# One more block product in seven smaller ones, and block sums carried in PSUM, in a mixer's channel layer

## The chip, the cores and the metric

The kernel runs on one core of a Trainium2 chip. Times are microseconds (us) of the device for one execution. The core has a matrix engine (TensorE, PE in the profile; its loading of the stationary operand is the row PEld), a vector engine (VectorE, DVE), a scalar engine (ScalarE, ACT), GpSimd (POOL) and SyncE (SP), which here only issues transfers (SPq is its queue). Matrix products are written into PSUM, which the program uses as four pairs of banks; a pair holds 128 rows of 1024 numbers. The other engines copy or add from there into SBUF.

## The reference, cut to what matters

```python
attn = ...                                        # attention within hash buckets, 4 x 8 heads, 768 rows of 64
x = attn.transpose(0, 2, 1, 3).reshape(4, 768, 512)
h = np.maximum(x.transpose(0, 2, 1) @ w_tok1, 0.0) @ w_tok2     # token mixing: 768 -> 256 -> 768
u = x + h.transpose(0, 2, 1)
h2 = np.maximum(u @ w_ch1, 0.0) @ w_ch2                         # channel mixing: 512 -> 1536 -> 512
return u + h2
```

Everything is in 32 bit floats. The change lies in the first product of the channel mixing, u @ w_ch1: 3072 rows of 512, to 1536 channels, and in the work around it.

## The kernel before

**Stages.** Attention, token mixing and channel mixing follow each other. The channel stage is the function `channels`. Its data lie turned: channels on the partitions, the 3072 rows of u along the free axis, in XT. They are treated in three column groups s = 0, 1, 2 of 1024 columns (two halves of TT = 512). For each group a hidden stage computes max(u @ w_ch1, 0) into four tiles R[0] to R[3], and then `outputs(s)` (L1260) computes the second product from R and stores it.

**Block products.** Each matrix product is cut in 2 x 2 blocks and done with seven block products in place of eight (the scheme of Strassen and Winograd): p1 and p2 to p7 are products of sums of left blocks (weights) with sums of right blocks (data), and the four results are sums of them:

- r0 = p1 + p2
- r1 = (p1 + p6) + p5 + p3
- r2 = (p1 + p6) + p7 + p4
- r3 = (p1 + p6) + p7 + p5

Sums of weights are made once and kept, in SW1 for the first product; sums of data are made by `inputs` (L601) into T[0] to T[3] (tiles TA and TB) for each group.

**The hidden stage of group 0** is `hidden(0, t)`, t = 0 to 5, one level of this. Between its steps run jobs that `prepare` (L1060) lists: VectorE makes sums of blocks of the weights for a second level, which SP stores in DRAM, in `hidden_passed` for the first product and `passed` for the second.

**The hidden stage of groups 1 and 2** is `hidden_pair(s, t, between)` (L932), t = 0, 1, 2 (GP = 3). Each takes a pair of row blocks, t and t + 3, of each of the two halves of the hidden channels. p1 and p5 are whole there: 4 products of 512 columns each (2 row blocks, 2 steps of depth, `whole`). p2, p6, p7, p3 and p4 are done on a second level, each with seven products of 128 x 128 by 128 x 256, by the class `Smaller` (L893). It has four parts:

- `one`: one product into a bank, and a copy of it into the first quarter of a tile e by ScalarE (L904)
- `three`: three products that go on top of what a bank pair holds already (or open it, where `start` is true)
- `rest`: three more in the bank of `one`
- `finish`: a copy of one product's sum by ScalarE to u (L925), and two sums by VectorE (L927, 128x512, and L930, 128x256), which fill the other three quarters of e

So a block product is a sum of two parts: one lies in the bank pair that `three` wrote, the other in e. The left operands of these seven come from `hidden_passed`, 448 KB for one block product of one pair (`fetch_hidden_left`, L862, issued on SP's queue as soon as the tile has been used for the pair before). The right ones are the raw blocks and four sums that a job of `right_sums` (L838) makes on VectorE, four subtractions of 128x256. They are made once per group: p2's and p6's ahead of the stage, the others at t = 0 in the list `between`.

ScalarE copies bank pairs out (`copy`, L960, 128x1024), VectorE adds (`plus`, L963), ScalarE applies the Relu to r0, r2 and r3 (L966), and r1 gets it in `bounded_minus` (L795), which also makes the difference r1 - r0 that the second product needs. The last of these lie in a list, which `end_rows` (L797) runs during the next pair.

**Looks.** `look` (L1338) belongs to a safety test of q and k. It fetches one 128x768 tile by POOL (L1355, 384 KB), and for the tile fetched some looks before it runs a square (L1344) and a bounded sum (L1345) on ScalarE. There are 36 in all; 12 in the hidden stage of each of groups 1 and 2 (four a pair), and one in each product of `outputs` of groups 0 and 1 (L1226).

**What sets the order.** The order of instructions is written out by hand (`tc.manual_schedule()`): each engine runs its instructions in the order of the code. An instruction waits for others through the tiles that both use. A PSUM tile here is a bank pair, and waits are made for the parts of it that two instructions touch, by bank. `ring` says which bank pair plays which part in a pair of rows, and `ahead` holds the bank pair in which the next step's first products have been begun: p1's of the next pair, or, at the end of a group's hidden stage, the first 8 of 12 depth steps of half of the whole product of `outputs` (`whole_first`, EARLY). That product (`whole_product`, L1182) is the first of `outputs`, 24 products of 256 columns.

The end of a pair, and the beginning of the next, read

```python
            if t + 1 < GP:
                ahead.append(bank_pair(y))
                opened(ahead[0], [0], t=t + 1)
```

where y is the bank pair from which `plus(r[1], banks(Y), rows(u))` reads p5 and p3.

**POOL and SP.** POOL issues the fetches of the looks and the stores of the results, which add to what is in DRAM (L1270). SP issues the fetches of the left operands, and `residual` (L1323) after t = 0, four transfers of 512 KB from XT to the output.

Of the kernel before, what the change touches and what calls it, by code (L numbers as in the profile page):

```python
# [48 lines left out]
def kernel(  # L49
# [702 lines left out]
    def channels(pool, psum, SW1, second, TA, judge):  # L752
# [85 lines left out]
        def right_sums(name, s):  # L838


            sl = [slice(TT * (2 * s + i), TT * (2 * s + i) + TT) for i in range(2)]
            src = {"p2": XT[:, KC:, sl[0]], "p3": XT[:, KC:, sl[1]], "p6": T[1], "p7": T[2], "p4": T[3]}[name]
            if name == "p7":
                z = SW1[:, 1].rearrange("p k c -> p (k c)")[:, : 2 * TT]
            else:
                z = XT[:, ["p2", "p6", "p3", "p4"].index(name), : 2 * TT]
            z = split4(z)
            half = [slice(0, TT // 2), slice(TT // 2, TT)]
            b = [src[:, k, n] for k in range(2) for n in half]

            def job():
                nc.vector.tensor_tensor(z[:, 0], b[1], b[0], op=ALU.subtract)
                nc.vector.tensor_tensor(z[:, 1], b[3], b[1], op=ALU.subtract)
                nc.vector.tensor_tensor(z[:, 2], b[3], z[:, 0], op=ALU.subtract)
                nc.vector.tensor_tensor(z[:, 3], b[2], z[:, 2], op=ALU.subtract)

            return job, [*b, *(z[:, i] for i in range(4))]
# [12 lines left out]

        def hidden_left_at(h):

            h, n = h % 5, 7 * P
            if h < 3:
                return WC1[:, KC:].rearrange("p k c -> p (k c)")[:, n * h : n * h + n]
            return SW1[:, 2 * (h - 3)].rearrange("p k c -> p (k c)")[:, :n]
# [5 lines left out]
        def first_weight(name):  # L882

            return {
                "p2": WC1[:, KC:, : DCH // 2], "p3": SW1[:, 2], "p4": WC1[:, KC:, DCH // 2 :], "p6": SW1[:, 0],
                "p7": SW1[:, 1],
            }[name]
# [5 lines left out]
        class Smaller:  # L893


            def __init__(self, h, name, s):
                self.h, self.w = h, hidden_left_at(h).rearrange("p (i c) -> p i c", i=7)
                self.b = right_sums(name, s)[1]

            def one(self, pair, e):  # L900

                self.ps, self.e = pair, split4(e)
                self.mm(pair[:, 0, : TT // 2], 4, 0)
                nc.scalar.copy(self.e[:, 0], pair[:, 0, : TT // 2])  # L904

            def three(self, pair, start=False):

                self.mm(pair[:, 0, : TT // 2], 5, 2, start)
                self.mm(pair[:, 0, TT // 2 :], 3, 3, False)
                self.mm(pair[:, 1, : TT // 2], 6, 7, start)  # L910

            def rest(self):

                self.mm(self.ps[:, 1, : TT // 2], 0, 4)
                self.mm(self.ps[:, 1, TT // 2 :], 1, 5)
                self.mm(self.ps[:, 0, : TT // 2], 2, 6, False)
                fetch_hidden_left(self.h + 5)

            def mm(self, ps, left, right, start=True):
                accumulate(ps, lambda k: self.w[:, left], lambda k: self.b[right], [0], start)  # L920

            def finish(self):

                u = extra_flat()[:, TT // 2 * (self.h % 2) : TT // 2 * (self.h % 2) + TT // 2]
                nc.scalar.copy(u, self.ps[:, 0, : TT // 2])  # L925
                p57 = self.ps[:, 1].rearrange("p (n t) -> p n t", n=2)
                nc.vector.tensor_tensor(  # L927
                    self.e[:, 1:3], p57, u[:, None, :].to_broadcast([P, 2, TT // 2]), op=ALU.add,
                )
                nc.vector.tensor_tensor(self.e[:, 3], p57[:, 0], self.e[:, 2], op=ALU.add)  # L930

        def hidden_pair(s, t, between):  # L932


            sl = [slice(TT * (2 * s + i), TT * (2 * s + i) + TT) for i in range(2)]
            ks = range(KC)
            r = [a[:, :, t::GP].rearrange("p n i c -> p i n c") for a in R]
            x, z, e, y = ring
            ring[:] = [y, e, z, x]

            p1, e2 = [output_at(i).rearrange("p i n -> p (i n)") for i in (0, 2)]
            p5, e6, u = copies(), copies(), copies()
            e3, e4 = [output_at(i).rearrange("p i n -> p (i n)") for i in (3, 1)]
            e7 = q1.rearrange("p i n -> p (i n)")
            h = 5 * GP * (s - 1) + 5 * t
            p2, p6, p7, p3, p4 = [Smaller(h + i, name, s) for i, name in enumerate(SMALLER)]

            def rows(a):
                return a.rearrange("p (i n c) -> p i n c", i=2, n=2)

            def banks(a):
                return a.rearrange("p i (n c) -> p i n c", n=2)

            def whole(pair, left, right, which=(0, 1), t=t):
                for i in which:
                    at = P * (t + GP * i)
                    accumulate(pair[:, i], lambda k: left(k)[:, at : at + P], right, ks)

            def copy(to, pair):
                nc.scalar.copy(to.rearrange("p (i n) -> p i n", i=2), pair)  # L960

            def plus(to, a, b):
                nc.vector.tensor_tensor(to, a, b, op=ALU.add)  # L963

            def relu(i):
                nc.scalar.activation(r[i], r[i], ACT.Relu)  # L966

            def opened(pair, which, s=s, t=t):
                start = TT * 2 * s
                whole(pair, lambda k: WC1[:, k], lambda k: XT[:, k, start : start + TT], which, t)  # L970

            X = ahead.pop() if ahead else None
            if not X:
                X = bank_pair(x)
                opened(X, [0])
            opened(X, [1])
            Z, E = bank_pair(z), bank_pair(e)
            p2.one(E, e2)
            copy(p1, X)
            p2.three(Z, True)  # L980
            Y = bank_pair(y)
            whole(Y, lambda k: WC1[:, k, DCH // 2 :], lambda k: T[0][:, k], [0])
            n = TT * 3 // 2
            plus(p1[:, :n], Z.rearrange("p i n -> p (i n)")[:, :n], p1[:, :n])
            for job in between[:2]:
                job()
            end_rows()
            p2.rest()
            whole(Y, lambda k: WC1[:, k, DCH // 2 :], lambda k: T[0][:, k], [1])
            p2.finish()  # L990
            copy(p5, Y)
# [3 lines left out]
            copy(u, X)  # L995
            look()
            V = bank_pair(e)
            p7.three(V, True)
            p6.rest()
            plus(p5[:, :n], V.rearrange("p i n -> p (i n)")[:, :n], p5[:, :n])  # L1000
            p6.finish()
            for job in between[2:]:
                job()
# [7 lines left out]
            relu(0)  # L1011
# [10 lines left out]
            if t + 1 < GP:  # L1022
                ahead.append(bank_pair(y))
                opened(ahead[0], [0], t=t + 1)
            else:
                ahead.append(blocks(1)[0])
                whole_first(s, ahead[0])
# [5 lines left out]
            look()  # L1033

            def end():
                relu(3)
                relu(2)
                for i in range(2):
                    bounded_minus(r[1][:, i], r[0][:, i])

            unfinished.append(end)


# [3 lines left out]
        ahead, EARLY = [], [k for k in range(HC) if k % GP < GP - 1]  # L1047
# [12 lines left out]
        def prepare():  # L1060
# [42 lines left out]
            def hidden_parts(name):  # L1103
# [6 lines left out]

            sums = weight_sums(WC2, SW2, slice(0, HC), slice(HC, NHT), low, high)
            return [
                [hidden_parts("p7")], sums, [whole("p1"), second_parts("p7")], *([second_parts(name)] for name in ("p6", "p3", "p5", "p2", "p4")),
                [hidden_parts("p2")], [hidden_parts("p6")], [hidden_parts("p3")], [hidden_parts("p4")],
# [59 lines left out]
        def whole_part(s, pair, m, ks, start=True, stop=True):  # L1174
            w, right = first_left(s), R[int(RIGHT["p1"][1])]
            accumulate(
                split(pair[:, m]), lambda k: w[:, k, P * m : P * m + P], lambda k: right[:, :, k], ks, start, stop,
            )

        def whole_first(s, pair):  # L1180
            whole_part(s, pair, 0, EARLY, stop=False)

        def whole_product(s):
            if ahead:
                pair = ahead.pop()
                whole_part(s, pair, 1, EARLY, stop=False)
                late = [k for k in range(HC) if k not in EARLY]
                for m in (1, 0):
                    whole_part(s, pair, m, late, False)
            else:  # L1190
                pair = blocks(1)[0]
                for m in range(KC):
                    whole_part(s, pair, m, range(HC))
# [4 lines left out]
        def product(s, j, name, q, between, final=None):  # L1198
# [27 lines left out]
            if s < last:  # L1226
                look()
# [165 lines left out]
        for s in range(1, last + 1):  # L1393
            right_sums("p6", s)[0]()
            for t in range(GP):
                hidden_pair(s, t, [right_sums(name, s)[0] for name in ("p7", "p3", "p4")] if t == 0 else [])
                if t == 0:
                    residual(s)
# [8 lines left out]
    def with_token_weights(stage):  # L1407
        with tc.tile_pool(name="tok", bufs=1, reuse_waits="tile") as tok:
# [10 lines left out]
            f"p{i}": dram.tile([P, 8, NHT // 4 * P], F32, name=f"hidden_left{i}") for i in (2, 3, 4, 6, 7)  # L1419
# [102 lines left out]
```

## Time and profile before

| What | us |
|---|---|
| median of 3 runs (793.72 to 794.22) | 794.18 |
| the profiled execution | 793.64 |
| its span, first to last instruction | 791.9 |
| attention | up to about 309 |
| token mixing | 309 to 387 |
| channel mixing | 387 to 792 |

The span is 1.7 us shorter than the profiled execution, which is itself 0.54 us below the median. The granted clock of TensorE is 0.999 over the span.

In what follows, a line of the timeline gives the start, the duration, the engine, the line of the code, the operation and its operands as out<-in with shapes; xN means N records that ran without a break. One product in 32 bit floats leaves two records. Where the engine had been idle, brackets at the end give that time and what ended it. A line of the groups gives the count, then the busy time in us and the mean duration of one in ns, and then the idle time ahead of these and what ended it. The chain of waits is the work that ended last, followed back from the end, here in order of time: start, duration, engine and line.

Three stretches of group 1's hidden stage, as windows of the trace. The columns are the stretch, its length, the busy time of PE, PEld, DVE, ACT and POOL with their instructions, the granted clock, the share of the DMA engines and GB/s:

```profile
525.00:547.50 22.50, 22.15 (x86) 15.98 (x85) 19.14 (x34) 12.54 (x23) 3.67 (x5) 1.00 0.86 241
547.50:569.50 22.00, 22.00 (x87) 16.36 (x87) 18.05 (x25) 16.68 (x29) 2.11 (x5) 1.00 0.90 288
569.50:591.50 22.00, 22.00 (x85) 15.96 (x84) 17.68 (x25) 16.57 (x29) 2.08 (x5) 1.00 0.60 177
```

### The profile page before, as it was taken

To read this page: it belongs to the slowest core of one execution; us is meant where nothing else is said; L and a number is where in the kernel's file an instruction comes from. 1 tells how busy PE (TensorE), PEld (TensorE's weight loads), DVE (VectorE), ACT (ScalarE), POOL (GpSimd) and SP (SyncE) were. 2 spreads that over 40 slices of the span, in tenths; PEclk is the share of its full clock that TensorE was granted. 3 is DMA by queue.
4 is the path that set the end of the run, shared out by engine and by line. 5 is a ranking of instruction groups with operands and counts; after the bars stand their busy time and mean duration, and the time that the engine had idled before them with its cause. 6 is when DMAs were issued, how large, how long until landed. Compare 5 with 4: busy or idle time off the path is not lost.

```text
span 791.9 us, 12326 instructions
## 1 busy us (share of the span) xinstructions
PE 784.5 (99%) x4697; PEld 471.3 (60%) x4697; DVE 674.5 (85%) x921; ACT 442.4 (56%) x718; POOL 53.5 (7%) x77
## 2 busy tenths in 40 slices
PE   9999999999999999999999999999999999999997
PEld 5444444444444444455544458877777887676886
DVE  5989898988987677999697689898879998888996
ACT  6788888888888886333323221327764335775111
POOL 1000000000000000011121010011100012000001
PEclk9999999999999999999999999999999999999999
DMA  4435353537452425795686995798856588650665
GB/s 164 163 123 163 123 163 123 163 127 240 154 180 83 151 44 168 219 264 107 119 280 235 346 333 163 202 294 238 264 163 208 180 219 190 211 171 1 195 166 123
DMA packets 99760, 143.01 MB, mean 181 GB/s; under 512 B 30120, under 2 KB 69744, under 8 KB 99696
## 3 DMA queue, kind: packets, MB, share of 16 engines
q1 hardware_dynamic: 91536, 117.19, 45.6%
q0 software_dynamic: 7728, 24.64, 14.0%
q8 instruction: 38, 0.62, 0.3%
q10 hardware_dynamic: 432, 0.34, 0.2%
q14 instruction: 26, 0.21, 0.1%
HBM read 99.96 MB, written 34.73 MB: 170 GB/s over the span
## 4 chain that ended last, share of the span: by engine, by line
PE 97%; DVE 2%; ACT 1%; issue 0%; DVEq 0%
PE b L780 48%; PE sc L353 20%; PE acc L407 16%; PE t L653 5%; PE t L693 5%; PE sums L431 2%; PE hp L301 1%; PE idle L470 0%; DVE R L963 0%; DVE c L963 0%; PE hw L325 0%; ACT looked L1345 0%; ACT c L960 0%; ACT looked L1344 0%; DVE c L927 0%; DVE q L927 0%
## 5 line engine op out<-in xcount | busy, mean ns | idle before, releaser
L360 ACT ACTIVATE e<-sc 128x768 f32<-128x768 f32 x192 | 154.2, 812 | 10.5 <-PE sc L353 10.1
L353 PE MATMUL sc<-qk 64*128 64x384 f32 x768 | 152.7, 483 | 0.0
L780 PE MATMUL b<-R,second 128*128 128x256 f32 (+1 forms) x612 | 151.2, 404 | 0.0
L780 PEld LDWEIGHTS b<-R,second 128*128 128x128 f32 x612 | 116.2, 190 | 30.8 <-issue 16.5
L786 ACT COPY c<-b 128x512 f32<-128x512 f32 (+1 forms) x78 | 37.4, 488 | 169.3 <-PE b L780 155.5
L407 PE MATMUL acc<-e,vn 128*32 128x384 f32 x1536 | 127.0, 486 | 0.0
L392 DVE TENSOR_TENSOR esd<-esd,e 128x768 f32<-128x768 f32 x96 | 92.0, 958 | 10.4 <-ACT e L360 0.5
L407 PEld LDWEIGHTS acc<-e,vn 128*32 128x32 f32 x1536 | 49.9, 110 | 73.9 <-issue 73.3
L353 PEld LDWEIGHTS sc<-qk 64*128 64x128 f32 x768 | 68.2, 187 | 41.2 <-issue 36.0
L780 PE MATMUL b<-XT,WC 128*128 128x256 f32 (+1 forms) x228 | 75.4, 470 | 0.7 <-DVE R L963 0.7
L353 PE MATMUL sc<-bits 64*128 64x384 bf16 x384 | 62.6, 323 | 0.0
L780 PEld LDWEIGHTS b<-XT,WC 128*128 128x128 f32 x228 | 43.2, 190 | 28.4 <-issue 22.2
L388 DVE SCALAR_TENSOR_TENSOR esd<-e 128x768 f32<-128x768 f32 x32 | 30.6, 956 | 23.3 <-ACT e L360 23.3
L780 PE MATMUL b<-XT,SW 128*128 128x256 f32 (+1 forms) x156 | 43.7, 412 | 0.0
L780 PE MATMUL b<-TA,WC 128*128 128x512 f32 (+1 forms) x108 | 43.6, 521 | 0.0
L653 PE MATMUL t<-x,W 128*128 128x512 f32 x96 | 41.8, 593 | 0.0
L353 PEld LDWEIGHTS <-bits 64*128 64x128 bf16 x384 | 18.7, 94 | 33.1 <-issue 8.8
L780 PEld LDWEIGHTS b<-XT,SW 128*128 128x128 f32 x156 | 29.6, 190 | 11.7 <-issue 6.8
L713 POOL DMA_DIRECT2D XT<-second x8 | 9.9, 1232 | 382.7 <-DVE second L712 355.1
L452 ACT COPY rec<-rec 32x384 f32<-32x384 f32 x64 | 32.6, 510 | 5.0 <-DVE rec L446 4.2
L413 ACT ACTIVATE num<-acc,vsum 128x384 f32<-128x384 f32 x32 | 18.6, 582 | 29.7 <-PE acc L407 29.3
L395 DVE TENSOR_TENSOR esd<-esd,e 128x768 f32<-128x768 f32 x32 | 30.5, 954 | 1.9
(226 smaller groups left out, 1155.8 us busy)
## 6 DMA issues: line engine op xcount, KB each, us to landing
second<-left SPq DMA_DIRECT2D x20, 768.0 KB
raw<-in_moe_w_ch SPq DMA_DIRECT2D x16, 768.0 KB
qk<-in_qk SPq DMA_DIRECT2D x15, 768.0 KB
second<-left SPq DMA_DIRECT2D x18, 576.0 KB
seen<-in_qk POOLq DMA_DIRECT2D x21, 384.0 KB, 4.3
WC<-hidden_left SPq DMA_DIRECT2D x18, 448.0 KB
vn<-in_v SPq DMA_DIRECT2D x16, 384.0 KB
vt<-in_vT SPq DMA_DIRECT2D x16, 384.0 KB
```

The costliest lines, as they stand in the source:

```text
L353: nc.tensor.matmul(sc[:, i, :HALF], t[rows, 1, P * c : P * c + P], t[rows, 0, qs], start=start, stop=not start,)
L360: nc.scalar.activation(e, sc[:, :, :HALF], ACT.Exp, scale=SCALE)
L388: nc.vector.scalar_tensor_tensor(self.d, es[0], NR * EPS, es[1], op0=ALU.add, op1=ALU.add,)
L392: nc.vector.tensor_tensor(self.d, self.d, e, op=ALU.add)
L395: nc.vector.tensor_tensor(self.d, self.d, self.es[-1], op=ALU.add)
L407: nc.tensor.matmul(acc[D * i + d : D * i + d + 32], vn[:, i, c, d : d + 32], e[:, i], start=(c == 0), stop=(c == NR - 1),)
L413: nc.scalar.activation(nums[self.n][:, self.half], acc, ACT.Identity, scale=-1.0, bias=vsum,)
L452: nc.scalar.copy(rec[other : other + 32, h], rec[at : at + 32, h])
L653: nc.tensor.matmul(ps, W1[:, r, P * j : P * j + P], x[:, r], start=(r == 0), stop=(r == NR - 1),)
L693: nc.tensor.matmul(ps[at], left, right, start=start, stop=True, skip_group_check=True,)
L780: nc.tensor.matmul(ps, left(k), right(k), start=start and k == ks[0], stop=stop and k == ks[-1], skip_group_check=True,)
L786: nc.scalar.copy(c, ps)
```

## The change

- In the pairs t = 1 and t = 2 of groups 1 and 2, p5 is done on the second level too, in seven products of 256 columns in place of four of 512. Three of its left operands are raw blocks of the weights; four sums are made by a new job of `prepare`, `fifth_parts`, during group 0, stored in a new piece of `hidden_passed`, and fetched by `fetch_fifth` (256 KB). Its right sums are made by one more `right_sums` job, at t = 0.
- These two pairs have a new order (`hidden_pair`). A sum of block products is written back into PSUM, and later products go on top of it: VectorE writes (p1 + p6) + e5, 128x1024, into the bank pair Y, on which `p5.three` and later `p3.three` accumulate. ScalarE writes the first quarter of p7's e into the bank pair V (in `one`) and, from SW1, the two middle quarters (128x512, at the end of `finish`), VectorE writes the last quarter there; `p7.three` and later `p4.three` accumulate on that. Y is copied to v after `p5.three` (`copy_pair`), and r3 is V + v.
- The pair t = 0 keeps its order as `hidden_first`, but p4's right sums move ahead of `p7.three`, and those of p5 come after the sum of p5 and p7. `end_rows` leaves it.
- `finish` takes its u from three places in turn, not two. Left operands are fetched anew after the second use of a tile, by `used`.
- The whole product of `outputs` is no longer begun in the hidden stage: `whole_part`, `whole_first` and EARLY go.
- The looks are spread otherwise: 4, 3 and 2 in the three pairs of a group, one per product in `outputs(0)` and two in `outputs(1)`; 36 as before.

The diff, cut to its core:

```diff
+            src = {"p2": XT[:, KC:, sl[0]], "p3": XT[:, KC:, sl[1]], "p5": T[0], "p6": T[1], "p7": T[2], "p4": T[3]}[name]
+            if name == "p5":
+                z = left_at(7 * s)[:, HC * 2 * P : HC * 2 * P + 2 * TT]
+            elif name == "p7":
                 z = SW1[:, 1].rearrange("p k c -> p (k c)")[:, : 2 * TT]
...
+        def fetch_fifth(s, t):
+
+            if t < GP:
+                nc.sync.dma_start(
+                    out=fifth_left().rearrange("p (i c) -> p i c", i=4),
+                    in_=hidden_passed["p5"][:, :, P * t : P * t + P],
+                )
+
+        def fifth_left():
+            return SW1[:, 1].rearrange("p k c -> p (k c)")[:, 2 * TT : 2 * TT + 4 * P]
+
...
+            def __init__(self, h, name, s, t):
+                self.h, self.s, self.t, self.fetched = h, s, t, False
                 self.b = right_sums(name, s)[1]
+                if name == "p5":
+                    raw = [a for b in weight_quarters(first_weight(name)) for a in b]
+                    raw = [raw[i][:, 0, P * t : P * t + P] for i in (0, 1, 3)]
+                    sums = fifth_left().rearrange("p (i c) -> p i c", i=4)
+                    self.left = [*(sums[:, i] for i in range(4)), *raw]
+                else:
+                    w = hidden_left_at(h).rearrange("p (i c) -> p i c", i=7)
+                    self.left = [w[:, i] for i in range(7)]
 
             def one(self, pair, e):
 
-                self.ps, self.e = pair, split4(e)
-                self.mm(pair[:, 0, : TT // 2], 4, 0)
-                nc.scalar.copy(self.e[:, 0], pair[:, 0, : TT // 2])
+                self.ps, self.e = split4(pair.rearrange("p i n -> p (i n)")), split4(e)
+                self.mm(self.ps[:, 0], 4, 0)
+                nc.scalar.copy(self.e[:, 0], self.ps[:, 0])
 
             def three(self, pair, start=False):
 
                 self.mm(pair[:, 0, : TT // 2], 5, 2, start)
                 self.mm(pair[:, 0, TT // 2 :], 3, 3, False)
                 self.mm(pair[:, 1, : TT // 2], 6, 7, start)
+                self.used()
 
             def rest(self):
 
-                self.mm(self.ps[:, 1, : TT // 2], 0, 4)
-                self.mm(self.ps[:, 1, TT // 2 :], 1, 5)
-                self.mm(self.ps[:, 0, : TT // 2], 2, 6, False)
-                fetch_hidden_left(self.h + 5)
+                self.mm(self.ps[:, 1], 0, 4, False)
+                self.mm(self.ps[:, 2], 1, 5)
+                self.mm(self.ps[:, 0], 2, 6, False)
+                self.used()
+
+            def used(self):
+
+                if self.fetched and self.h is None:
+                    fetch_fifth(self.s, self.t + 1)
+                elif self.fetched:
+                    fetch_hidden_left(self.h + 5)
+                self.fetched = True
 
             def mm(self, ps, left, right, start=True):
-                accumulate(ps, lambda k: self.w[:, left], lambda k: self.b[right], [0], start)
-
-            def finish(self):
-
-                u = extra_flat()[:, TT // 2 * (self.h % 2) : TT // 2 * (self.h % 2) + TT // 2]
-                nc.scalar.copy(u, self.ps[:, 0, : TT // 2])
-                p57 = self.ps[:, 1].rearrange("p (n t) -> p n t", n=2)
+                accumulate(ps, lambda k: self.left[left], lambda k: self.b[right], [0], start)
+
+            def finish(self, middle=None):
+
+                u = extra_flat()[:, TT // 2 * finished[0] : TT // 2 * (finished[0] + 1)]
+                finished[0] = (finished[0] + 1) % 3
+                nc.scalar.copy(u, self.ps[:, 0])
+                to = self.e[:, 1:3] if middle is None else split(middle)
                 nc.vector.tensor_tensor(
-                    self.e[:, 1:3], p57, u[:, None, :].to_broadcast([P, 2, TT // 2]), op=ALU.add,
+                    to, self.ps[:, 1:3], u[:, None, :].to_broadcast([P, 2, TT // 2]), op=ALU.add,
                 )
-                nc.vector.tensor_tensor(self.e[:, 3], p57[:, 0], self.e[:, 2], op=ALU.add)
+                nc.vector.tensor_tensor(self.e[:, 3], self.ps[:, 1], to[:, 1], op=ALU.add)
+                if middle is not None:
+                    nc.scalar.copy(self.e[:, 1:3], to)
...
+        def open_next(bank, s, t):
+            ahead.append(bank_pair(bank))
+            opened(ahead[0], [0], s, t + 1)
+
+        def later(r, which):
+
+            def end():
+                for i in which:
+                    relu(r[i])
+                for i in range(2):
+                    bounded_minus(r[1][:, i], r[0][:, i])
+
+            unfinished.append(end)
+
...
+        def hidden_first(s, t, between):
...
             X = bank_pair(x)
             opened(X, [0, 1], s, t)
             fetch_fifth(s, t + 1)
...
             for job in between[:2]:
                 job()
-            end_rows()
             p2.rest()
...
             look()
             V = bank_pair(e)
+            between[2]()
             p7.three(V, True)
             p6.rest()
             plus(p5[:, :n], flat(V)[:, :n], p5[:, :n])
+            between[3]()
             p6.finish()
-            for job in between[2:]:
-                job()
             plus(u, u, e6)
...
             p4.one(bank_pair(x), e4)
             look()
             nc.scalar.copy(r[2][:, 1, 1], rows(u)[:, 1, 1])
-            if t + 1 < GP:
-                ahead.append(bank_pair(y))
-                opened(ahead[0], [0], t=t + 1)
-            else:
-                ahead.append(blocks(1)[0])
-                whole_first(s, ahead[0])
+            open_next(y, s, t)
             p4.rest()
...
             look()
+            later(r, (3, 2))
...
+        def hidden_pair(s, t):
+
+
+            r, (p2, p6, p7, p3, p4) = parts_of(s, t)
+            p5 = Smaller(None, "p5", s, t)
+            one, two, three, four = ring
+            e2, e4, e5, e3 = [flat(output_at(i)) for i in range(4)]
+            e6 = flat(q1)
+            p1, u, v = copies(), copies(), copies()
+            n = TT * 3 // 2
+
+            X = ahead.pop()
+            p2.one(bank_pair(three), e2)
+            opened(X, [1], s, t)
+            p6.one(bank_pair(two), e6)
+            copy_pair(p1, X)
+            p2.rest()
+            p6.rest()
+            p2.finish()
+            p6.three(X)
+            p6.finish()
+            look()
+            p5.one(bank_pair(three), e5)
+            plus(u, flat(X), e6)
+            Z = bank_pair(four)
+            p2.three(Z, True)
+            plus(p1[:, :n], flat(Z)[:, :n], p1[:, :n])
+            V = bank_pair(four)
+            p7.one(bank_pair(two), flat(V))
+            p5.rest()
+            p5.finish()
+            p3.one(bank_pair(one), e3)
+            Y = bank_pair(three)
+            plus(flat(Y), e5, u)
+            p7.rest()
+            p7.finish(flat(SW1[:, 0])[:, 7 * P : 7 * P + TT])
+            if t + 1 < GP:
+                look()
+            plus(r[0], rows(p1), rows(e2))
+            p3.rest()
+            p3.finish()
+            p5.three(Y)
+            copy_pair(v, Y)
+            p7.three(V)
+            p4.one(bank_pair(two), e4)
+            relu(r[0])
+            plus(r[3], banks(V), rows(v))
+            p3.three(Y)
+            p4.rest()
+            relu(r[3])
+            plus(r[1], banks(Y), rows(e3))
+            p4.finish()
+            look()
+            p4.three(V)
+            plus(e4, e4, u)
+            end_rows()
+            plus(r[2], banks(V), rows(e4))
+            if t + 1 < GP:
+                open_next(one, s, t)
+            else:
+                ring[:] = [one, three, two, four]
+            later(r, (2,))
...
+            def fifth_parts():
+                (a00, a01), (a10, a11) = weight_quarters(first_weight("p5"))
+                n = QC * P
+                pieces = [flat(q1)[:, : 2 * n], pool.tile([P, S], F32, name="looked", tag="looked", bufs=1)]
+                new = [a[:, n * i : n * i + n].rearrange("p (k c) -> p k c", k=1) for a in pieces for i in range(2)]
+                nc.vector.tensor_tensor(new[1], a00, a10, op=ALU.subtract)
+                nc.vector.tensor_tensor(new[0], a10, a11, op=ALU.add)
+                nc.vector.tensor_tensor(new[2], new[0], a00, op=ALU.subtract)
+                nc.vector.tensor_tensor(new[3], a01, new[2], op=ALU.subtract)
+                for i, a in enumerate(pieces):
+                    to = hidden_passed["p5"].rearrange("p i c -> p (i c)")
+                    nc.sync.dma_start(out=to[:, 2 * n * i : 2 * n * i + 2 * n], in_=a[:, : 2 * n])
+
...
-                [hidden_parts("p2")], [hidden_parts("p6")], [hidden_parts("p3")], [hidden_parts("p4")],
+                [hidden_parts("p2"), fifth_parts], [hidden_parts("p6")], [hidden_parts("p3")], [hidden_parts("p4")],
...
+        def whole_product(s):
+            pair = blocks(1)[0]
             w, right = first_left(s), R[int(RIGHT["p1"][1])]
-            accumulate(
-                split(pair[:, m]), lambda k: w[:, k, P * m : P * m + P], lambda k: right[:, :, k], ks, start, stop,
-            )
-
-        def whole_first(s, pair):
-            whole_part(s, pair, 0, EARLY, stop=False)
-
-        def whole_product(s):
-            if ahead:
-                pair = ahead.pop()
-                whole_part(s, pair, 1, EARLY, stop=False)
-                late = [k for k in range(HC) if k not in EARLY]
-                for m in (1, 0):
-                    whole_part(s, pair, m, late, False)
-            else:
-                pair = blocks(1)[0]
-                for m in range(KC):
-                    whole_part(s, pair, m, range(HC))
+            for m in range(KC):
+                accumulate(
+                    split(pair[:, m]), lambda k: w[:, k, P * m : P * m + P], lambda k: right[:, :, k], range(HC),
+                )
...
-            if s < last:
+            for _ in range(min(s + 1, 2) if s < last else 0):
                 look()
...
-            for t in range(GP):
-                hidden_pair(s, t, [right_sums(name, s)[0] for name in ("p7", "p3", "p4")] if t == 0 else [])
-                if t == 0:
-                    residual(s)
+            hidden_first(s, 0, [right_sums(name, s)[0] for name in ("p7", "p3", "p4", "p5")])
+            residual(s)
+            for t in range(1, GP):
+                hidden_pair(s, t)
```

## The prediction

> **What bounds the kernel now.** I read the head of the page, then the chain of waits in order of time, then the timeline around its breaks.
>
> ```profile
> span 791.9 us, 12326 instructions
> PE 784.5 (99%) x4697; PEld 471.3 (60%) x4697; DVE 674.5 (85%) x921; ACT 442.4 (56%) x718; POOL 53.5 (7%) x77
> ```
>
> TensorE is busy for 99% of the span. A product removed is worth its time only if no other engine is then late.
>
> ```profile
> 386.83 148.42 PE b L780 x482
> ...
> 541.26 1.14 DVE c L963
> 543.46 1.14 DVE R L963
> ...
> 544.65 121.83 PE b L780 x492
> ```
>
> This is the channel stage's chain: one stretch of TensorE up to 535 us, then ScalarE and VectorE until 544.65, then TensorE for 122 us. The break returns in the third column group (675.88) and nowhere else. The timeline shows it:
>
> ```profile
> 535.54 1.02 ACT L960 COPY c<-b 128x1024 f32<-128x1024 f32 x1
> 536.45 0.86 ACT L1344 ACTIVATE looked<-looked 128x768 f32<-128x768 f32 x1
> 536.64 0.96 DVE L963 TENSOR_TENSOR c<-b,c 128x768 f32<-128x768 f32 x1 [1.54 <-ACT c L960]
> ...
> 538.27 0.35 ACT L925 COPY second<-b 128x256 f32<-128x256 f32 x1
> ...
> 538.65 0.69 DVE L927 TENSOR_TENSOR c<-b,second 128x512 f32<-128x512 f32 x1 [1.06 <-ACT second L925]
> ...
> 541.18 1.22 DVE L963 TENSOR_TENSOR c<-c 128x1024 f32<-128x1024 f32 x1
> ...
> 543.38 1.21 DVE L963 TENSOR_TENSOR R<-b,c 128x1024 f32<-128x1024 f32 x1
> ...
> 543.71 0.59 PE L780 MATMUL b<-TB,SW 128*128 128x256 f32 x2
> ...
> 544.65 1.98 PE L780 MATMUL b<-XT,WC 128*128 128x512 f32 x4 [0.35 <-DVE R L963]
> ```
>
> PE's product of 543.71 is done with its slot at 544.14 (0.43 us), and the next starts at 544.65: 0.5 us lost, because the sum into R reads the bank that p1 of t=1 opens. VectorE was late although it had idled 1.54 and 1.06 us just before. One look holds ScalarE for 1.82 us (536.45 to 538.27). The prices, grouped by shape in the channel stage:
>
> ```profile
> L780 PE MATMUL b<-XT,SW 128*128 128x256 f32 x132 | 32.4, 379 | 0.0
> L966 ACT ACTIVATE R<-R 128x1024 f32<-128x1024 f32 x18 | 18.9, 1061 | 3.7 <-DVE R L963 3.7
> L927 DVE TENSOR_TENSOR second<-b,second 128x512 f32<-128x512 f32 x18 | 12.3, 686 | 4.5 <-ACT second L925 4.5
> L960 ACT COPY c<-b 128x1024 f32<-128x1024 f32 x12 | 12.2, 1017 | 8.1 <-PE b L780 8.1
> L930 DVE TENSOR_TENSOR second<-b,second 128x256 f32<-128x256 f32 x18 | 7.6, 424 | 0.6
> L963 DVE TENSOR_TENSOR c<-c 128x1024 f32<-128x1024 f32 x6 | 7.3, 1223 | 0.1
> L963 DVE TENSOR_TENSOR R<-b,c 128x1024 f32<-128x1024 f32 x6 | 7.3, 1214 | 0.0
> L904 ACT COPY second<-b 128x256 f32<-128x256 f32 x18 | 6.7, 372 | 9.8 <-PE b L780 8.6 <-DMA out<-second 0.6
> ```
>
> PE's pitch comes from the timeline: 44 records of 256 columns from 556.80 to 566.29, two to a product, are 0.43 us per product. A 512 column product takes 0.86.
>
> **The change part by part.**
>
> Products removed: p5 was 4 products of 512 columns, 8 units of 0.43, and becomes 7. Two pairs (t=1, 2) in two column groups: 4 x 0.43 = **-1.72 us**. All of it lies on PE's path.
>
> Breaks removed: at t=0 the sums for p4 (4 subtractions, 539.72 to 541.26) move ahead of VectorE's wait of 1.54 us, and the new ones for p5 (the same 1.5 us) fill the 1.06 us wait. The 128x1024 sum that began at 541.18 begins about 1.06 us earlier, so the sum into R ends near 543.5, ahead of 544.14. Both 0.5 us breaks go: **-1.0 us**. Next late there is nothing within 0.5 us.
>
> Waits added. In t=1 and t=2 the order is new, and results now return to PSUM before TensorE may go on. I walk the PE units against the other two engines.
>
> (a) Start of t=1. p2's second part now adds to the bank whose first quarter ScalarE copies. With S the start of p4's last product of t=0: ScalarE's copy begins at S+0.64 (0.43, and 0.2 from a product's end to a copy, as the copy at 540.88 after the products that end at 540.68 shows), the look at S+0.92, p2's copy at S+2.74, and it ends at S+3.11. TensorE has p2's first product, two of 512 and p6's first: S+3.01. With a hand-over of 0.05 it waits **0.15**.
>
> (b) p7's second part adds to the bank pair V. There VectorE writes a quarter, and then ScalarE copies the 128x512 middle in; that copy waits for VectorE's write. From the start of p5's last product in `rest` (0): copy of u 0.64 to 1.01; VectorE's finish of p5, 0.69 and 0.42, to 2.19; the sum written into Y, 1.22, to 3.43; p7's finish, 0.69 and 0.42, to 4.50; the copy, 0.59, from 4.57 to 5.16; PE at 5.21 (hand-overs of 0.02 to 0.07). TensorE's own work until then is 11 units (p5's last, p3's first, p7's three, p3's three, p5's second three), 4.75. It waits **0.46**. p5's second three need Y at 3.43 and come at 3.45: just met; a longer chain would show there first, not on top.
>
> (c) At t=1 ScalarE does a look right after that copy is begun: look from 5.06 to 6.88, p3's copy of u to 7.15 (next start), copy of Y to v 1.02, to 8.17. p3's second part adds to Y and waits for that: 8.22. TensorE, released at 5.21, has 4 units until then, 6.93. It waits **1.29**. Behind it stand p3, p4 and the next pair on PE; VectorE waits with them for p3's u.
>
> (d) t=2 has (b) again, **0.46**, but no look there: from 4.57 the copies take 0.50, 0.27 and 1.02 to 6.36, ahead of 6.93.
>
> One column group: 0.15 + 0.46 + 1.29 + 0.46 = 2.36; two: **+4.72**.
>
> Unknown prices: no row of before has VectorE or ScalarE writing PSUM. Reading it makes no difference (VectorE 1.214 against 1.223 us; ScalarE 1.017 from PSUM against 1.061 for the Relu without PSUM). I take the same duration as to SBUF, since those rows are nearest. The far ends are plus and minus 0.2 each, the largest gap between two engines' rows of one size (1.02 to 1.22). Three such writes lie in each of (b) and (d). Upward that gives up to 4 x 0.6 = +2.4 us; downward the waits can only vanish, 4 x 0.46 = -1.84.
>
> The Trainium skill, Perfetto Trace Analysis, "Optimizing Scalar/DVE Operations", gives VectorE about 60 ns of access overhead on SBUF and 125 on PSUM, and ScalarE 93 and 51. The rows above show no such step for VectorE's reads. By the page, as an estimate, the chain of (b) would be 2 x 0.065 - 0.042 = 0.09 us longer, four times: +0.35 on the total. PSUM — Partial Sum Buffer, "Summary: rules for kernel authors", says that an accumulation seeded by VectorE or ScalarE must have seed 0 on this chip, and its rules send other seeds through TensorE. That speaks against this change: two seeds of 1024 columns by matmul would, as an estimate, be 8 units, 3.4 us a pair, 13.8 us in all. The diff has no such matmuls, and no row here shows a seeded bank.
>
> Costed at nothing: the four sums of weights and two stores at the end of the first group's stage (about 2.2 us of VectorE and 768 KB) lie beside 3 to 4 us waits of VectorE for PE. VectorE's sums of t=1 and 2 fall by about 1 us a pair (two long sums fewer, one finish more) and ScalarE loses a look and two. DMA: the order on SP gains a 256 KB fetch per pair, issued long before use; p6's sums at t=1 land some 4 us ahead of need by the 6.4 us that the like transfer took (537.86 to 544.3). Looks moved into the second group's outputs find ScalarE 25.04 of 68.50 us busy (591.5 to 660); POOL's store after them, landed at 670.27 before, has until about 676, when a copy takes its place. The whole product, no longer half done in the hidden stage, keeps its 24 units; these 10.3 us cover VectorE's last 1.22, 1.37 and 1.37 us sums, so PE does not wait. If that cover were gone the price would be some of these 4 us, twice.
>
> Sum: -1.72 - 1.0 + 4.72 = **+2.0 us**. On the profiled execution, 793.64 us (span 791.9, 1.7 around it): 795.64. The median of the runs is 0.54 higher, 794.18, so **796.2**.
>
> **Rivals.**
>
> 1. Not slower: the chain of (b) and (d) is shorter. Its place is the return of p7's middle into V. From 0.1 us less a time, 4 x 0.1 takes the sum to +1.6, which is no measurable change (0.2%, 1.59 us, is about what the measurement tells from none); at 0.46 both waits are gone and +0.16 is left. For it: the margin is one unit, and ScalarE's row from PSUM is the shorter one. Against it: four of its seven steps have rows of their own kind. 794.3 to 795.8.
>
> 2. The products and breaks pay as they are meant to: the look is not in the way at (c) either. Sum -2.72 + 2 x 0.15, **791.8**; with (b) and (d) kept 793.6. Against it: ScalarE is in order and the look stands between the two copies.
>
> 3. PSUM writes are dearer than SBUF ones, by 0.07 to 0.2 each: +0.8 to +2.4 more, 797.0 to 798.6. VectorE's rows for reads speak against it.
>
> 4. A transfer is late: the stretch before the first break already has a DMA share of 0.83 to 0.9, a fetch of 448 KB took 6.4 us in it, and 256 KB and more are added to the same queue. If it takes 5 us more, p6 waits 1 us in each group, and the following fetches with it: 798 to 800. Against it: those 4 us, and a share of 0.60 from 569.5 to 591.5.
>
> **How the numbers follow.** The forecast, 795.8 to 796.9, has 0.42; rival 1 has 0.32; 2 has 0.08; 3 has 0.12; 4 has 0.06. Slower: 0.42 + 0.12 + 0.06, less 0.03 for the forecast's lower edge, 0.57. Within: 0.32, that 0.03 and 0.02 of rival 2 (793.6), 0.37. Faster: 0.06 of rival 2. The range leaves out rival 2, rival 4 and the top half of 3, 0.20 together: 794.2 to 798.0.
>
> **What would show it.** In the profile after: no idle time of PE at the end of t=0; in the waits, PE on ScalarE's copy of the middle, about 0.46 us four times, and on the copy of the bank pair Y, about 1.3 us twice, with the two rows of a look just before it; 128x1024 and 128x256 sums with a bank as output at 1.22 and 0.42 us. In these pairs the 512 column products of p5 are gone and 7 of 256 stand there. Rival 1 shows no PE wait on the middle; 3 shows longer rows; 4 shows PE waiting for a DMA. The prediction is wrong if the waits on a bank are narrower than the whole bank (then (b) and (d) vanish) or if the ends of products as modelled hide a wait.

## The result, and the profile after

| | before | after |
|---|---|---|
| median, us (7 runs each) | 794.06 | 796.48 |
| lowest to highest | 793.23 to 794.59 | 796.03 to 797.04 |
| ratio, 95% interval | | 1.0033 (1.0021 to 1.0045) |
| span of the profiled execution | 791.9 | 794.5 |
| channel stage on TensorE | 399.51 | 401.88 |

The kernel is slower by 2.4 us. The last row is taken from the chain of waits, and I use it for every kernel below: the end of the chain's last piece of channel products less the start of its first. It leaves out what differs from one execution to the next in front of the stage (its start lies between 386.7 and 387.9 us in the eight profiles) and the transfers behind its last product.

The profile after, from the head of the page:

```profile
PE 785.4 (99%) x4721; PEld 475.2 (60%) x4721; DVE 677.3 (85%) x929; ACT 441.9 (56%) x722; POOL 53.4 (7%) x77
```

The share of TensorE says nothing again: 99%. The chain of waits in order of time does (start, length, engine, line):

```profile
387.06 170.63 PE b L780 x576
...
563.08 1.03 ACT seen L1443 x2
...
582.74 1.23 DVE b L981
...
585.12 0.60 ACT b L963
...
752.66 36.28 PE b L780 x168
```

752.66 + 36.28 - 387.06 is the 401.88 of the table; in the kernel before it is 749.93 + 36.41 - 386.83 = 399.51. The break at 544 is gone: the first piece runs through it to 557.7. In its place TensorE leaves the chain twice in group 1: at t=1, where the chain comes by a look (L1443) and by the copy of Y that stands behind it (L984, in the waits below), and at t=2, where it comes by a sum with a bank as output (`DVE b L981`) and by the copy of p7's middle. Group 2 does the same 132 us later. The waits of TensorE and of its weight loads, from 470 us on:

```profile
PE b L780 <- ACT c L984: 2.0, 2, 1.0
...
PEld b L780 <- ACT b L963: 2.0, 4, 0.5
PEld b L780 <- PE b L780: 1.4, 4, 0.4
```

L984 is the copy of Y to v, twice; L963 the copy of p7's middle into PSUM, four times. The third line is not in the prediction, and the timeline of t=1 in group 1 explains it:

```profile
549.57 0.59 PE L780 MATMUL b<-TB,WC 128*128 128x256 f32 x2
...
549.66 0.35 ACT L925 COPY second<-b 128x256 f32<-128x256 f32 x1
...
550.07 2.86 PE L780 MATMUL b<-XT,WC 128*128 128x256 f32 x12
...
556.22 1.46 PE L780 MATMUL b<-second,SW 128*128 128x256 f32 x6
...
559.02 1.27 PEld L780 LDWEIGHTS b<-XT,SW 128*128 128x128 f32 x6
559.24 1.46 PE L780 MATMUL b<-XT,SW 128*128 128x256 f32 x6
559.30 1.23 DVE L981 TENSOR_TENSOR b<-second,c 128x1024 f32<-128x1024 f32 x1
...
560.65 0.30 PEld L780 LDWEIGHTS b<-TA,WC 128*128 128x128 f32 x2 [0.36 <-PE b L780]
560.68 0.67 PE L780 MATMUL b<-TA,WC 128*128 128x256 f32 x2
...
561.68 0.59 ACT L963 COPY b<-SW 128x512 f32<-128x512 f32 x1 [1.87 <-DVE b L961]
...
562.21 0.84 ACT L1442 ACTIVATE seen<-seen 128x768 f32<-128x768 f32 x1
...
562.32 0.73 PEld L780 LDWEIGHTS b<-TA,WC 128*128 128x128 f32 x4 [0.51 <-ACT b L963]
562.32 1.13 PE L780 MATMUL b<-TA,WC 128*128 128x256 f32 x4
...
564.26 1.01 ACT L984 COPY c<-b 128x1024 f32<-128x1024 f32 x1
...
565.33 2.86 PE L780 MATMUL b<-XT,SW 128*128 128x256 f32 x12 [1.01 <-ACT c L984]
```

Read it by TensorE's slots of 0.43 us. At the start of t=1, p6's first product (549.57) is through at 550.00; p2's copy behind a look ends at 550.01, and TensorE goes on at 550.07: a wait of 0.07, (a). p3's three products that start at 559.24 are through at 560.53, when VectorE's sum into Y ends; TensorE starts on Y at 560.68, 0.15 later. p7's second three wait for the copy of 561.68 and start at 562.32, 0.27 after the slot before them ends (562.05). p3's second three start at 565.33, behind the look and two copies, 1.18 after 564.15.

One thing more is in the rows: after each wait the next products take longer than their slots. The product of 560.68 is followed by the next at 561.18, 0.50 in place of 0.43; the two of 562.32 by the next at 563.29, 0.97 in place of 0.86. The rows of the weight loads (PEld) show where this comes from: a load otherwise starts about 0.22 ahead of its product of 256 columns (559.02 and 559.24), and behind a wait it starts 0.03 ahead (560.65 and 560.68) or together with it (562.32). That the late load is the cause is read from these rows; no run tests it by itself. The price is 0.07 to 0.11 after every wait, also after the two breaks before (0.10: from 544.65, four records took 1.98, and the same four in the kernel after, from 544.37 and without a wait, 1.88).

The sum of it, for one column group:

| place | predicted | measured (wait + slow start) |
|---|---|---|
| products, two pairs (counted in slots) | -0.86 | -0.86 |
| break before t=1 | -0.50 | -0.61 (0.51 + 0.10) |
| (a) start of t=1 | 0.15 | 0.18 (0.07 + 0.11) |
| (b) t=1, Y and the middle | 0.46 | 0.60 (0.15 + 0.07, 0.27 + 0.11) |
| (c) t=1, copy of Y behind the look | 1.29 | 1.29 (1.18 + 0.11) |
| (d) t=2, Y and the middle | 0.46 | 0.61 (0.15 + 0.07, 0.28 + 0.11) |
| sum | 1.00 | 1.21 |

Two groups give +2.42; the stage grew by 2.37, the median by 2.42. The rows are those of group 1, taken twice.

Three rows whose like the kernel before does not have, grouped by shape:

```profile
L981 DVE TENSOR_TENSOR b<-second,c 128x1024 f32<-128x1024 f32 x4 | 4.9, 1232 | 0.1
...
L961 DVE TENSOR_TENSOR b<-b,SW 128x256 f32<-128x256 f32 x4 | 1.7, 432 | 0.1
...
L925 ACT COPY b<-b 128x256 f32<-128x256 f32 x4 | 1.4, 357 | 6.8 <-DVE c L981 4.9 <-PE b L780 1.9
```

Writing PSUM costs VectorE 1.232 and 0.432 us, where the same sums into SBUF cost 1.223 and 0.424: 0.008 more. ScalarE's copies of 256 columns into PSUM (L925) take 0.357, where the kernel before, copying into SBUF, has 0.368 to 0.372.

### The profile page after: what moved, and what is told of

It reads as the page before. It is cut to its first block, busy times and chain, and to the rows that moved or that the text cites. A ratio compares the mean times of both kernels' runs of the same rounds, so it can differ in the third digit from the quotient of the medians.

```text
span 794.5 us, 12402 instructions
## 1 busy us (share of the span) xinstructions
PE 785.4 (99%) x4721; PEld 475.2 (60%) x4721; DVE 677.3 (85%) x929; ACT 441.9 (56%) x722; POOL 53.4 (7%) x77
## 3 DMA queue, kind: packets, MB, share of 16 engines
q0 software_dynamic: 7728, 24.64, 13.8%
## 4 chain that ended last, share of the span: by engine, by line
PE 96%; DVE 2%; ACT 1%; issue 0%; ACTq 0%; DVEq 0%
PE b L780 47%; PE sc L353 20%; PE acc L407 16%; PE t L653 5%; PE t L693 5%; PE sums L431 2%; PE hp L301 1%; DVE b L981 0%; PE idle L470 0%; DVE second L958 0%; DVE SW L958 0%; PE hw L325 0%; ACT b L963 0%; ACT seen L1443 0%; ACT second L956 0%
## 5 line engine op out<-in xcount | busy, mean ns | idle before, releaser
L780 PE MATMUL b<-TA,WC 128*128 128x256 f32 (+1 forms) x92 | 34.0, 479 | 0.4
```

The source lines that it names most:

```text
L780: nc.tensor.matmul(ps, left(k), right(k), start=start and k == ks[0], stop=stop and k == ks[-1], skip_group_check=True,)
```

## The experiments

My theory: products and breaks pay what the prediction says, and four kinds of wait take more than that back. The wait (c) is the look's, and (b) and (d) are the chain through p7's middle; at t=1 both lie on one path of ScalarE. Rivals are in the expectations. The first four kernels were measured beside one set of runs of the kernel before (median 793.98), the last two beside another (793.96). The changed kernel was not run again beside them: what is said against it, or of one of these kernels against another, goes by the length of the stage, from one profile of each. The edits change the order of work; the last two also make two PSUM tiles one.

### The look moved away from t=1

```diff
             p7.finish(flat(SW1[:, 0])[:, 7 * P : 7 * P + TT])
-            if t + 1 < GP:
-                look()
             plus(r[0], rows(p1), rows(e2))
...
-            for _ in range(min(s + 1, 2) if s < last else 0):
+            for _ in range(min(s + 1, 2) + (s == 0 and j in (1, 2)) if s < last else 0):
                 look()
```

> The changed kernel, but the look of t=1 that ScalarE does right after the copy of p7's middle is done elsewhere: one more look in each of the first two products of the first column group's outputs, none here. Theory: that look is what holds the copy of the bank pair Y to v, so the wait of 1.29 us (1.18 and 0.11 behind it) goes in both column groups: 2.6 us less than the changed kernel, 0.2 us or so from the kernel before (793.9); the waits on the middle's copy stay at 0.27 four times. Rival A: TensorE would wait for p3's or V's data there anyway: under 1 us less. Rival B: ScalarE's look costs the same where it is moved to: no change, 796.5.

Measured: 793.97, ratio to the kernel before 1.000 (0.9991 to 1.0009). The first and the last of the chain's pieces in the channel stage:

```profile
387.78 170.62 PE b L780 x576
...
750.83 36.28 PE b L780 x168
```

The stage takes 750.83 + 36.28 - 387.78 = 399.33, 2.55 less than after; 2.6 was expected. What ScalarE does at t=1 now:

```profile
562.40 0.59 ACT L963 COPY b<-SW 128x512 f32<-128x512 f32 x1 [1.87 <-DVE b L961]
...
563.19 1.02 ACT L984 COPY c<-b 128x1024 f32<-128x1024 f32 x1
```

p3's copy of u stands between the two. The copy of Y begins 0.79 us after the middle's, where it began 2.58 after it (561.68 to 564.26). So the look is the cause of (c), and rivals A and B fall. The place of this one line decides between a slower kernel and one that cannot be told from before.

### p4's first product ahead of p7's second three

```diff
-            p7.three(V)
             p4.one(bank_pair(two), e4)
+            p7.three(V)
```

> The changed kernel, but p4's first product (one unit of 0.43 us) is issued ahead of p7's second three instead of behind them. Theory: the wait on the middle's copy (0.28 and 0.11 behind it) is covered by that unit at t=1 and t=2, but at t=1 ScalarE's look and copies set when p3's second part may start, so what is gained there is given back: only t=2 gains, 2 x 0.39 = 0.8 us less than the changed kernel (795.7), and the wait for Y's copy at t=1 grows from 1.2 to 1.6. Rival: the waits are independent and add up: 4 x 0.39 = 1.5 us less (795.0).

Measured: 795.91, ratio to the kernel before 1.0027 (1.0017 to 1.0038). The stage takes 751.55 + 36.28 - 386.71 = 401.12, 0.76 less than after, where 0.8 was expected and the rival said 1.5. TensorE's products at t=1 in it:

```profile
562.13 1.03 PE L780 MATMUL b<-TA,WC 128*128 128x256 f32 x4
...
562.99 0.59 PE L780 MATMUL b<-SW,WC 128*128 128x256 f32 x2
...
564.97 1.35 PE L780 MATMUL b<-XT,SW 128*128 128x256 f32 x5 [1.39 <-ACT c L984]
```

p4's product, at 561.69, covers the middle's copy, and p7's products follow at 562.13 without a wait. But the slot of 562.99 ends at 563.42, and the next starts at 564.97: the wait on Y's copy grew from 1.18 to 1.55. ScalarE sets when p3's second part starts, and what TensorE wins ahead of it is lost there.

### Both

The two edits together.

> Both edits, the look away from t=1 and p4's first product ahead of p7's second three. Theory: now both waits go everywhere, 2.6 + 4 x 0.39 = 4.1 us less than the changed kernel, 792.4, which is 1.7 less than the kernel before; left are the waits for VectorE's write of Y (0.15 and 0.07, four times) and at the start of t=1 (0.18, twice). Rival: something else is late next (VectorE's sums or a fetch): between 793.0 and 795.0.

Measured: 792.64, ratio to the kernel before 0.9983 (0.9974 to 0.9992). The chain has one piece for nearly the whole stage:

```profile
387.94 361.41 PE b L780 x1368
749.46 36.28 PE b L780 x168
```

749.46 + 36.28 - 387.94 = 397.80: 4.08 less than after, 4.1 expected. The four waits at Y remain. They do not break the piece, because a product's row ends later, as modelled, than its slot: in the kernel after, the row of 559.24 ends at 560.70, and the product that had to wait starts at 560.68. The gain of both is 0.77 more than the sum of each (2.55 + 0.76), as the shared path says.

### The kernel before, with p4's sums ahead

```diff
             V = bank_pair(e)
+            for job in between[2:]:
+                job()
             p7.three(V, True)
...
             p6.finish()
-            for job in between[2:]:
-                job()
             plus(u, u, e6)
```

> The kernel before, but p4's right sums at t=0 (four subtractions on VectorE) are issued ahead of p7's first three products and of the sum of p5 and p7, into VectorE's wait of 1.54 us. Nothing else. Theory: the two breaks before t=1 (0.51 and 0.10 behind it, in two column groups) go: 1.2 us less than the kernel before, 792.9. So this much of the change is had without it. Rival: the breaks come from the look that holds ScalarE's copy for p6's finish, whatever VectorE does in between: no change, 794.1.

Measured: 792.74, ratio 0.9985 (0.9976 to 0.9994).

```profile
386.79 361.76 PE b L780 x1344
748.66 36.41 PE b L780 x168
```

The stage takes 398.28, 1.23 less than before (1.2 expected), and the breaks are gone, although the look still stands ahead of the copy for p6's finish; the rival falls. Moving four subtractions by some lines, without the seven products, gives a median of 792.74, where the changed kernel with both edits has 792.64; the two medians cannot be told apart. Between the two kernels lies p5 in seven products, with the new order and the other places of the looks that go with it: 397.80 - 398.28 = -0.48. Worked out it is -1.72 for the products, +0.88 for Y (4 x 0.22) and +0.36 for (a): -0.48. No run takes these terms one by one.

### One PSUM tile for p5 and Y

```diff
-            p5.one(bank_pair(three), e5)
+            F = bank_pair(three)
+            p5.one(F, e5)
...
-            Y = bank_pair(three)
+            Y = F
             plus(flat(Y), e5, u)
```

This stands on top of both edits.

> The kernel with both edits (look away, p4's first product first), and p5's bank pair and the bank pair Y made one PSUM tile (the same banks as before), so that TensorE's first product on Y waits for VectorE's write alone and not for an older product of its own as well. There TensorE starts 0.15 us after VectorE's row ends, where it starts 0.05 after ScalarE's in the other places. Theory A: the 0.15 comes from the second wait; then it falls to about 0.06, 4 x 0.1 = 0.4 us less than with both edits (792.2). Theory B: a sum written by VectorE into PSUM is seen that much later by TensorE: 0.15 stays, no change (792.6). The row of the write itself stays 1.23 us in both.

Measured: 792.37, ratio to the kernel before 0.9978 (0.9969 to 0.9987). The rows at Y:

```profile
559.35 1.23 DVE L981 TENSOR_TENSOR b<-second,c 128x1024 f32<-128x1024 f32 x1
...
560.63 0.30 PEld L780 LDWEIGHTS b<-TA,WC 128*128 128x128 f32 x2 [0.29 <-DVE b L981]
560.64 0.70 PE L780 MATMUL b<-TA,WC 128*128 128x256 f32 x2
```

VectorE's row ends at 560.58 and TensorE starts 0.06 later, so theory A holds for the delay: it came from the second wait, on an old product of TensorE's own, and not from the place of the write. The weight load says the same: here it waits for VectorE's sum, in the changed kernel for a product. The time fell by only half of what I expected: the next product comes at 561.17, so the first now takes 0.53 in place of 0.50, the slow start having grown from 0.07 to 0.10. The load's row goes with this: the next product comes 0.53 to 0.54 after the start of the load in both kernels (560.65 and 561.18, 560.63 and 561.17), and the load starts 0.05 after VectorE's row in place of 0.12, which is 0.07 and not 0.09 sooner. The stage takes 748.42 + 36.28 - 387.11 = 397.59, 0.21 less. The medians (792.64 and 792.37) agree with that, but could not show it alone.

### The last look of t=0 moved too

```diff
             plus(r[2], r[2], rows(e4))
-            look()
             later(r, (3, 2))
...
-            for _ in range(min(s + 1, 2) + (s == 0 and j in (1, 2)) if s < last else 0):
+            for _ in range(min(s + 1, 2) + (s == 0 and j in (1, 2, 3, 4)) if s < last else 0):
```

> As the run before it, and the last look of t=0 is moved to the first group's outputs too (three more looks there in two products' place, four in all). Theory: the wait at the start of t=1 (0.07 and 0.11, in two column groups) goes: 0.36 us less, 791.8 under theory A, 792.2 under B; 1.8 to 2.2 us less than the kernel before. Rival: p2's copy there is late for another reason than the look: no change against the run before it. Left of the change's cost would be only TensorE's 0.06 to 0.22 us at Y, four times.

Measured: 792.00, ratio to the kernel before 0.9974 (0.9964 to 0.9984).

```profile
387.26 360.85 PE b L780 x1368
748.22 36.28 PE b L780 x168
```

The stage takes 397.24, 0.35 less than the run before it; 0.36 expected, so the look was what held p2's copy. Four waits on Y are left, 0.06 + 0.10 each, 0.64 in all.

This kernel does the same work as the changed one, with four looks and one product in other places and one PSUM tile fewer, and is faster than both kernels: 2.0 us under before, 4.5 under after. Against the kernel before with p4's sums ahead, the stage is 1.04 shorter (397.24 and 398.28); the two were not run side by side. Where the looks went, in the first group's outputs, ScalarE is busy for 20.84 us of 64 (456 to 520), and TensorE has no gap.

## Why the prediction was right or wrong

- The time, 796.48, lies 0.3 from the forecast of 796.2, and the forecast's sign and place of each wait are in the profile. That it is so near is in part luck: the waits cost 0.64 us more than forecast (0.06 in (a), 0.28 in (b), 0.30 in (d), for two groups), the breaks gave back 0.22 more, and the median of the kernel before was 794.06, not 794.18.
- **Products, -1.72**: no run has it alone; the step from the kernel with p4's sums ahead to the one with both edits closes with it (-0.48, worked out and measured).
- **Breaks, -1.0**: right in cause (VectorE's order, shown by moving the four subtractions), undersized by 0.2. The term was 0.5 each; it is 0.61, because the slow start behind the break (0.10) was not counted.
- **(a) 0.15**: 0.18 measured, but put together otherwise, 0.07 of wait and 0.11 of slow start. The look as its cause is shown.
- **(b) and (d), 0.46**: the chain's end was placed at 5.21 us after p5's last product and is at 5.24 (557.08 to 562.32). The term was mis-sized by 0.14 and 0.15 each. The step "just met" at Y was wrong: TensorE started 0.15 late there. That wait itself adds nothing, as the prediction said, since the chain sets the end behind it; what adds is the slow start of 0.11 behind the last wait and 0.03 of the chain.
- **(c) 1.29**: 1.29 measured, as 1.18 of wait and 0.11 of slow start; the look as its cause is shown. The equal sums are chance: TensorE came to this wait 0.14 late, at 7.07 for 6.93, since its slow start behind the middle was not forecast, and so waited less; the slow start behind this wait made up for it.
- **The price of writing PSUM**, taken as that of SBUF: right to 0.008 us a sum. The Trainium skill (Perfetto Trace Analysis, "Optimizing Scalar/DVE Operations") gives VectorE an overhead of about 60 ns on SBUF and 125 on PSUM; by that, as an estimate, each would have been 0.065 longer. The rows of this case show 0.008 for writes, and no step for reads. The page PSUM — Partial Sum Buffer of the skill ("Summary: rules for kernel authors") says that the seed must be 0; the prediction's estimate for other seeds sent through TensorE was 13.8 us. The changed kernel writes its seeds by VectorE and ScalarE without such matmuls: it has 24 PE records more (4721 against 4697), two for each of the three more products of four pairs. On what it depends whether such a seed is added to, no run here shows.
- **Rivals 1 to 4**: the waits at the middle are there, 0.60 and 0.61 together with those at Y, though on the middle's copy itself TensorE waits 0.27 and not 0.46 (against 1); the look is in the way (against 2); PSUM writes are dearer by 0.008 only (against 3); the profile has no wait of TensorE for a transfer in the stage (against 4).
- **Costed at nothing**: the sums and stores in group 0 and the whole product not begun early left no gap on TensorE, by the chain: its pieces on TensorE run from 387.06 to 557.69, which has group 0, and from 585.76 to 690.16 and from 718.24 to the end of the stage, which have the whole products of groups 1 and 2.
- What the prediction did not see is how little stood between the two signs: it named the look as the largest term, and did not say that the look has free room elsewhere.

## What to carry to other kernels

When results are written back into PSUM for later products to add on, each such hand-back is a round trip over one or two other engines, and has to be walked slot by slot against the products that are left in between; here one unit of other work (0.43 us) in the right place covered a wait of 0.27. Optional work on an engine that is idle for much of the time (ScalarE is busy for 56% of the span) still does harm right in front of a copy that the busy engine waits for, and two waits on one path have to be mended together. A wait that is cured by reordering alone (here 1.23 us) should be taken out first, so that the larger rewrite is judged without it.

## What the runs showed that I had not expected

- A wait costs TensorE more than its length: the products behind it take 0.07 to 0.11 us longer, and the rows show their weights loaded with them and not ahead. At six waits a column group that is 0.6 us.
- Where TensorE had to wait on two things (another engine's sum and an older product of its own), it started 0.15 us after the later one, and 0.06 with a single wait, but 0.03 of that gain went into a longer start.
